# Routing attention with a spectral gate: the first mask made head by head, fewer idle products, and a new order of instructions

## The chip, the core and the metric

The kernel runs on one core of a Trainium2 chip. A core has five engines with instruction queues of their own: TensorE (PE, matrix products), VectorE (DVE), ScalarE (ACT), GpSimd (POOL) and SyncE (SP, which here only starts transfers). Sixteen DMA engines move data. Products land in PSUM, which has eight banks of 128 rows by 2 KB; everything else lies in SBUF. Each engine takes its instructions in the order in which they stand in the program, and an instruction that needs another engine's result waits for a semaphore. The metric is the device time of one execution in microseconds (us); lower is better. "Profile" means one execution recorded by the hardware profiler.

## What is computed

The reference, cut to what matters:

```python
q_assign = argmax(einsum('bhsd,hcd->bhsc', q_n, c_n), -1)     # 16 centroids per head
k_assign = argmax(einsum('bhsd,hcd->bhsc', k_n, c_n), -1)
mask = q_assign[:, :, :, None] == k_assign[:, :, None, :]
scores = where(mask, q @ k.T / sqrt(64), -1e9)
attn = exp(scores - max);  attn = attn / (attn.sum(-1) + 1e-9)
x = (attn @ v)                                                # (4, 768, 8 * 64)
x1, x2, x3 = split(x @ w_proj, 3)                             # 512 -> 3 * 512
y = x1 * irfft(rfft(x2) * rfft(filter)) * x3                  # along the sequence
out = y @ w_out                                               # (4, 768, 512) float32
```

There are 4 batches, 8 heads, 768 positions and 64 numbers per head. Every position is given to the nearest of 16 centroids, for its query and for its key; a query sees only the keys with the same centroid.

## The kernel before

The work is cut into eight groups n of four heads (batch n // 2, half n % 2), and each group into two pairs pr of two heads hp. `routing(n)` turns q and k of a group so that the 64 numbers of a head lie along the rows, multiplies with the normed centroids, takes the argmax, and makes a one-hot row block: 16 rows, one per centroid, which stand beside the 64 rows of q or k in the operands of the scores. With these rows a product of q and k comes out hugely negative where the centroids differ, so that the mask costs no work of its own. These operands are the tiles `aug`: `aug_97` is head 0 and `aug_98` head 1 of the first pair, `aug_99` and `aug_100` belong to the second pair, `aug_101` and `aug_102` to the third; then the three are used again in turn. In each, j = 0 is the query side and j = 1 the key side.

`attention(n, pr)` runs over six blocks sk of 128 keys. For each there are three score products ("thirds" of 512 columns: the first is head 0 alone, the second half of each head, the third head 1 alone; lines 156 and 158), three exponentials on ACT into a tile `p` (lines 690 and 693), one group of eight products with v (line 704), and a running sum of `p` for the denominator (lines 713 and 717, DVE or POOL). When two groups of a batch are done, `hyena` makes the projection, the spectral filter as products with cosine tables, the gates and the output product (lines 158, 455 and 838).

The first pair is a case of its own, `first_masks(0)`. Its start goes so: two waves of transfers bring q and k (line 295); PE turns them by products with the identity `ident` (line 602, three per PSUM bank); ACT or DVE copies each bank to `qkP` (lines 246 and 248 are the helper that copies); four products with the centroid matrix `cbd` give the similarities (line 502); ACT copies them to `sim`; PE turns them back (line 511); DVE takes the argmax in five instructions over 24 groups of 16 (lines 518 to 525: maximum, equal to it, times a falling weight so that the first of equal ones wins, maximum, equal to it), into the one-hot tile `oh`; PE turns this into rows (line 535) in two banks, one for j = 1 and one for j = 0, each with both heads; and four copies `put` (line 546 or the helper) write the rows to `aug_97` and `aug_98`. The bodies of q and k come to `aug` by the casts of `routing` on ACT, DVE or POOL. The second pair takes the same five instructions once more (`first_masks(1)`), then six turns (line 555), one write to `sim` (line 558) and four transfers by SP (line 487).

Before its first real product, PE runs idle products on a tile of ones (`warm`, with `awake` as one product, line 1101): ten ahead of everything, and one more ahead of each of the eight turns of the first group.

The order of all this isn't found at run time. `build` records each step as an `Op` with the engines that may do it, what it reads and what it writes. `arrange` then walks through the list `ORDER`: each number stands for a step (number // 5) and the engine that does it (number % 5), and the steps are issued in that order. `due` and the costs in an `Op` don't move anything here; only the list does. `arrange` also gives out the PSUM banks, the first free ones of its list, and decides by the step before whether a product is issued whole or as two halves of 64 columns. A step marked `lock` on POOL waits for the last step marked so on DVE.

## Time and profile before

| | us |
|---|---|
| median of 3 runs | 348.03 |
| lowest and highest run | 347.56, 348.55 |
| the profiled execution | 348.1 |
| its span, from the first to the last instruction | 346.3 |
| PE busy in the span | 336.8 |
| DVE busy | 327.6 |
| ACT busy | 274.2 |
| POOL busy | 135.1 |
| first exponential starts | 16.52 |
| first product with v starts | 19.62 |

A row of the timeline has the start in us, the length in us, the engine, the line, the operation and "out<-in" with the shape; "x3" means that three instructions are merged, and a bracket gives the idle time of the engine just ahead of it with what ended it. "PEld" is a weight load on TensorE, "SPq" and "ACTq" are the starts of transfers. Where two rows of an engine overlap a little, the next instruction entered while the one before was still finishing. In the table of stages each engine has its busy time with the number of instructions, then the granted clock of TensorE, the share of the DMA engines and their rate.

### The profile page before, as it was taken

To read this page: it belongs to the slowest core of one execution; us is meant where nothing else is said; L and a number is where in the kernel's file an instruction comes from. 1 tells how busy PE (TensorE), PEld (TensorE's weight loads), DVE (VectorE), ACT (ScalarE), POOL (GpSimd) and SP (SyncE) were. 2 spreads that over 40 slices of the span, in tenths; PEclk is the share of its full clock that TensorE was granted. 3 is DMA by queue.
4 is the path that set the end of the run, shared out by engine and by line. 5 is a ranking of instruction groups with operands and counts; after the bars stand their busy time and mean duration, and the time that the engine had idled before them with its cause. 6 is when DMAs were issued, how large, how long until landed. Compare 5 with 4: busy or idle time off the path is not lost.

```text
span 346.3 us, 8366 instructions
## 1 busy us (share of the span) xinstructions
PE 336.8 (97%) x3164; PEld 194.7 (56%) x3165; DVE 327.6 (95%) x438; ACT 274.2 (79%) x509; POOL 135.1 (39%) x161
## 2 busy tenths in 40 slices
PE   8899999999999999999999999999999999999994
PEld 4464465454455556655665656676455555576672
DVE  6899999999999999999999999999999999989992
ACT  7999999999799989887898797697998655524442
POOL 6423407004115447234702686126501161336740
PEclk9999999999999999999999999999999999999998
DMA  8979986775799997798969776998748321500124
GB/s 184 195 150 208 181 168 125 123 152 122 161 160 157 141 169 89 153 117 185 142 124 167 132 126 150 195 135 128 164 103 142 72 25 43 173 5 2 74 110 184
DMA packets 132052, 46.19 MB, mean 133 GB/s; under 512 B 119192, under 2 KB 124140, under 8 KB 132012
## 3 DMA queue, kind: packets, MB, share of 16 engines
q1 hardware_dynamic: 127884, 35.79, 49.9%
q0 software_dynamic: 2752, 8.98, 18.7%
q10 hardware_dynamic: 1376, 0.89, 0.8%
q8 instruction: 25, 0.41, 0.5%
q14 instruction: 15, 0.12, 0.1%
HBM read 31.59 MB, written 7.40 MB: 113 GB/s over the span
## 4 chain that ended last, share of the span: by engine, by line
PE 81%; ACT 8%; DVE 8%; issue 1%; ACTq 0%; DVEq 0%
PE bank L158 38%; PE pair L704 32%; PE bank L838 5%; PE bank L622 3%; DVE acc L717 2%; ACT aug L246 1%; PE bank L733 1%; DVE tm L868 1%; PE bank L455 1%; ACT p L693 1%; ACT qkP L246 1%; ACT sim L648 1%; DVE ohB L637 1%; DVE oh L635 1%; DVE mx L633 1%
## 5 line engine op out<-in xcount | busy, mean ns | idle before, releaser
L704 PE MATMUL pair<-p,vraw 128*64 128x385 f32 x768 | 142.1, 487 | 0.0
L693 ACT ACTIVATE p<-bank 128x512 f32<-128x512 f32 x192 | 108.6, 606 | 22.5 <-PE bank L158 19.8
L717 DVE TENSOR_TENSOR acc<-p,acc 128x1536 f32<-128x1536 f32 x64 | 112.9, 1765 | 2.6 <-ACT p L693 0.2
L158 PE MATMUL bank<-aug 128*64 128x512 bf16 (+1 forms) x738 | 83.7, 327 | 0.3 <-ACT p L693 0.2
L704 PEld LDWEIGHTS pair<-p,vraw 128*64 128x64 f32 x768 | 57.9, 136 | 42.6 <-issue 33.7
L158 PEld LDWEIGHTS <-aug 128*64 128x64 bf16 (+1 forms) x738 | 45.0, 109 | 36.7 <-issue 25.3
L754 POOL DMA_DIRECT2D acc<-acc x30 | 23.9, 796 | 98.4 <-DVE acc L717 61.4
L690 ACT ACTIVATE p<-bank 128x512 f32<-128x512 f32 x96 | 57.1, 609 | 5.4 <-PE bank L158 4.3
L158 PE MATMUL bank<-xT,wpj 128*64 128x384 bf16 x504 | 49.4, 326 | 0.0
L158 PEld LDWEIGHTS <-wpj 128*64 128x64 bf16 x504 | 30.9, 110 | 14.4 <-issue 4.6
L246 ACT CAST aug<-qkP 64x768 bf16<-64x768 f32 x46 | 37.7, 829 | 0.8
L713 POOL TENSOR_TENSOR acc<-p,p 128x1536 f32<-128x1536 f32 x7 | 24.3, 3474 | 29.6 <-DVE acc L717 27.8
L158 PEld LDWEIGHTS <-y 128*64 128x64 bf16 x488 | 24.6, 110 | 12.7 <-issue 4.1
L868 DVE TENSOR_TENSOR tm<-bank,hm 128x512 f32<-128x512 f32 x44 | 27.9, 681 | 1.1 <-PE bank L455 0.5
L158 PE MATMUL bank<-wout,y 128*64 128x512 bf16 (+1 forms) x200 | 23.9, 371 | 0.2 <-DVE y L964 0.2
L579 DVE STREAM_TRANSPOSE qkP<-qkraw 128x768 f32<-128x768 f32 x26 | 24.0, 953 | 0.0
L838 PE MATMUL bank<-wpj,xT 128*64 128x512 bf16 x192 | 22.8, 379 | 0.4 <-ACT tm L246 0.4
L872 POOL TENSOR_TENSOR y<-tm 128x512 bf16<-128x512 f32 x15 | 19.0, 1274 | 10.6 <-DVE tm L868 8.2
L964 POOL TENSOR_TENSOR y<-yy,x 128x768 bf16<-128x768 f32 x9 | 16.4, 1827 | 15.1 <-DVE acc L717 7.1
L246 ACT COPY x<-bank 128x384 f32<-128x384 f32 x27 | 13.1, 484 | 11.4 <-PE bank L158 10.6
L246 ACT COPY ob<-bank 128x512 f32<-128x512 f32 x22 | 12.8, 589 | 11.1 <-PE bank L158 9.4
L248 POOL CAST aug<-qkP 64x768 bf16<-64x768 f32 x15 | 12.5, 840 | 17.7 <-DVE acc L717 7.4
(175 smaller groups left out, 415.0 us busy)
## 6 DMA issues: line engine op xcount, KB each, us to landing
rb<-dr SPq DMA_DIRECT2D x30, 192.0 KB, 3.5
qkraw<-in_k_dram SPq DMA_DIRECT2D x55, 96.0 KB, 3.2
qkraw<-in_q_dram SPq DMA_DIRECT2D x55, 96.0 KB, 3.2
vraw<-in_v_dram SPq DMA_DIRECT2D x52, 96.0 KB, 3.2
out_dram<-ob SPq DMA_DIRECT2D x9, 512.0 KB, 3.2
acc<-acc POOLq DMA_DIRECT2D x10, 384.0 KB, 5.2
acc<-acc POOLq DMA_DIRECT2D x10, 192.0 KB, 4.0
y<-in_moe_filter_fft_dram SPq DMA_DIRECT2D x4, 384.0 KB, 4.9
```

The costliest lines, as they stand in the source:

```text
L158: T.nc.tensor.matmul(out[64 * i:64 * i + 64], lhsT[:, 64 * i:64 * i + 64], rhs, start=start, stop=stop)
L246: T.nc.scalar.copy(out, in_)
L579: op(("DVE", .96), lambda e, s=s, z=z, j=j: V().transpose(T.qkP[z // 2][:, ts(j, S)], T.qkraw[s][:].rearrange("p t h d -> p (t h d)") if j ...
L690: T.nc.scalar.activation(o, ap(h).rearrange("p (a b) -> p a b", a=2), Act.Exp, scale=0.125)
L693: T.nc.scalar.activation(flat(s)[:, lo:lo + 512], ap(h), Act.Exp, scale=0.125)
L704: T.nc.tensor.matmul(o[64 * hp:64 * hp + 64, ch, :385], T.vraw[vs][:, hp, sk * D:(sk + 1) * D], T.p[slots[sk]][:, hp, 384 * ch:384 * ch + ...
L713: alu(e).tensor_tensor(T.acc[os], T.p[slots[0]][:, :, :S], T.p[slots[1]][:, :, :S], op=Alu.add)
L717: T.nc.vector.tensor_tensor(T.acc[os], T.p[slots[sk]][:, :, :S], T.acc[os], op=Alu.add)
L754: op(("POOL", .8), lambda e, rows=rows: T.nc.gpsimd.dma_start(flat_()[:rows], flat_()[rows:2 * rows], accum_op=Alu.add), te, r=[], w=AK, b ...
L838: T.nc.tensor.matmul(ap(h)[64 * i:64 * i + 64], T.xT[xs][:, kt, c:c + 64], T.wpj[:, kt, DM:2 * DM], start=kt == 0, stop=kt == ND - 1)
L868: op(("DVE", .68), lambda e, i=i, cs=cs, r=r, h=h: T.nc.vector.tensor_tensor(T.tm[r][:, cs], ap(h), hmrow(i, (0, 2, 2, 3)[2 * r + cs]), op ...
L872: op({"POOL": 1.5, "DVE": .68}, lambda e, i=i, r=r: alu(e).tensor_tensor(T.y[:, i, r], T.tm[r][:, 0], T.tm[r][:, 1], op=Alu.add if r else ...
```

## The change

The change has four parts.

The argmax of the first pair is cut by heads. In place of five DVE instructions over 24 groups there are ten over 12 groups, five for each head; every second group belongs to a head (`hp::2`). The turns to rows are cut likewise: four banks of six products in place of two of twelve, so that each bank holds one head and one j. There are still four `put` copies.

The idle products are cut: `WARM` is 8 in place of 10, and the first four turns (query and key of the first pair, `z` 0 and 1) have no idle product ahead of them. Of 18 idle products 12 are left.

The keys of `mx` and `oh` are now per head for the first pair, and `both` in `routing` names all of them. This only keeps the dependencies right.

`ORDER` is a new list over the whole program, since the steps have new numbers and stand in another order. It also gives some steps to another engine: in all, ACT has 41 casts to `aug` in place of 46, DVE none in place of 2, and POOL 22 in place of 15; ACT has 3 of the zero fills of `aug` (line 1074, now 1080) in place of 1, and POOL 3 in place of 5; one `put` is on ACT, where all four were on DVE.

```diff
 ORDER = [
-    2, 179, 106, 28, 5, 171, 23, 32, 154, 161, 184, 18, 48, 169, 13, 98, 159, 37, 62, 51, 206, 66, 58, 267, 189, 272, 277, 149, 43, 112, 236, 117,
+    2, 154, 106, 13, 18, 5, 181, 159, 166, 98, 62, 149, 23, 164, 28, 37, 822, 179, 51, 103, 236, 267, 58, 207, 189, 76, 272, 277, 174, 66, 112, 43,
...
-WARM = 10
+WARM = 8
...
-        bc = lambda a: a.unsqueeze(2).to_broadcast([128, 24, NC])
-        op(("DVE", .55), lambda e: V().tensor_reduce(mx(), sv(), axis=AX, op=Alu.max), due + .5, r=[h], w=[("mx", pr)])
...
+        put_ = []
+        for hp in range(2) if pr == 0 else (None,):
+            N = 24 if hp is None else 12
+            k = ((pr,) if hp is None else (pr, hp))
+            part = (lambda x: x) if hp is None else (lambda x, hp=hp: x[:, hp::2])
+            bc = lambda a, N=N: a.unsqueeze(2).to_broadcast([128, N, NC])
+            D_ = (.55, .36) if hp is None else (.36, .26)
+            dd = due + .5 * (hp or 0)
+            op(("DVE", D_[0]), lambda e, part=part: V().tensor_reduce(part(mx()), part(sv()), axis=AX, op=Alu.max), dd + .5, r=[h], w=[("mx", *k)])
+            op(("DVE", D_[0]), lambda e, part=part, bc=bc: V().tensor_tensor(part(oh()), part(sv()), bc(part(mx())), op=Alu.is_equal), dd + .6,
+               r=[h, ("mx", *k)], w=[("oh", *k)], free=[h])
...
+            for j in (1, 0) if pr == 0 else ():
                 h2 = Bank("head")
-                def rows(e, j=j, h2=h2):
+                def rows(e, j=j, hp=hp, h2=h2):
                     o = ap(h2).bitcast(BF16)
                     for t in range(NT):
-                        for hp in range(2):
-                            T.nc.tensor.transpose(o[64 - 64 * hp:80 - 64 * hp, ts(t, 128)], oh()[:, at(t) + 2 * j + hp], T.identb)
+                        T.nc.tensor.transpose(o[64 - 64 * hp:80 - 64 * hp, ts(t, 128)], oh()[:, at(t) + 2 * j + hp], T.identb)
...
-                def tr(e, s=s, ch=ch, j=j, h=h):
-                    if n == 0:
+                def tr(e, s=s, ch=ch, z=z, h=h):
+                    if n == 0 and z > 1:
                         awake(h)
...
-        both = lambda x: [(x, 0), (x, 1)]
+        both = lambda x: [(x, 0, 0), (x, 0, 1), (x, 1)]
```

The new list shows in the instructions at three places. In these rows the line numbers of the changed kernel are higher (602 is 608, 502 stays, 518 is 525, 535 is 540, 546 is 551, 555 is 561, 693 is 699, 704 is 710). The names `bank_63` to `bank_68` and `bank_153`, `bank_154` are PSUM banks.

On DVE, the argmax of the first pair and the writes of its rows, before, up to the argmax of the second pair:

```order
L518 TENSOR_REDUCE mx<-bank_65 128x24
L519 TENSOR_TENSOR oh<-bank_65,mx 128x384
L521 TENSOR_TENSOR oh<-oh,revc 128x384
L523 TENSOR_REDUCE m_87<-oh 128x24
L525 TENSOR_TENSOR oh<-oh,m_87 128x384
L248 CAST aug_98<-qkP_113 64x768
L546 TENSOR_SCALAR aug_97<-bank_68 16x768
L248 COPY aug_97<-bank_153 16x768
L546 TENSOR_SCALAR aug_98<-bank_68 16x768
L518 TENSOR_REDUCE mx<-bank_154 128x24
L248 COPY aug_98<-bank_153 16x768
L519 TENSOR_TENSOR oh<-bank_154,mx 128x384
```

and after:

```order
L525 TENSOR_REDUCE mx<-bank_65 128x12 x2
L526 TENSOR_TENSOR oh<-bank_65,mx 128x12x16 x2
L528 TENSOR_TENSOR oh<-oh,revc 128x12x16 x2
L530 TENSOR_REDUCE m_87<-oh 128x12
L532 TENSOR_TENSOR oh<-oh,m_87 128x12x16
L530 TENSOR_REDUCE m_87<-oh 128x12
L532 TENSOR_TENSOR oh<-oh,m_87 128x12x16
L551 TENSOR_SCALAR aug_98<-bank_68 16x768
L551 TENSOR_SCALAR aug_97<-bank_154 16x768
L248 COPY aug_97<-bank_63 16x768
L525 TENSOR_REDUCE mx<-bank_66 128x24
L526 TENSOR_TENSOR oh<-bank_66,mx 128x384
```

The two heads go side by side up to the weighting; then head 1 (`aug_98`) is finished first and head 0 (`aug_97`) second. One cast and one of the four writes have left this stretch of DVE.

On ACT, from the copy of the first pair's similarities to the first exponential, before:

```order
L246 COPY sim<-bank_154 128x384
L246 CAST aug_97<-qkP_113 64x768
L373 ACTIVATE fw<-tm_136 128x2x192
L246 COPY qkP_114<-bank_63 128x384
L246 COPY qkP_114<-bank_66 128x384
L246 COPY qkP_114<-bank_64 128x384
L373 ACTIVATE fw<-tm_137 128x2x192
L246 CAST aug_100<-qkP_114 64x768
L246 COPY sim<-bank_67 128x384
L368 ACTIVATE ob_139<-tm_137 128x384
L693 ACT_TABLE_LOAD
L693 ACTIVATE p_103<-bank_66 128x512
```

and after:

```order
L246 COPY sim<-bank_154 128x384
L373 ACTIVATE fw<-tm_136 128x2x192
L375 ACTIVATE wout<-ob_138,half_pi 128x2x192
L373 ACTIVATE fw<-tm_137 128x2x192
L246 COPY qkP_114<-bank_66 128x384
L246 COPY qkP_114<-bank_67 128x384
L368 ACTIVATE ob_139<-tm_137 128x384
L246 CAST aug_100<-qkP_114 64x768
L246 COPY sim<-bank_64 128x384
L246 COPY aug_98<-bank_153 16x768
L699 ACT_TABLE_LOAD
L699 ACTIVATE p_103<-bank_67 128x512
```

One cast and one copy have left the stretch, one table of sines (line 375) and the write of head 1's key rows have come in.

On PE, the turns of the first pair up to the turn of the centroids, before (the rows of ten idle products ahead are left out):

```order
L1101 MATMUL bank_64<-wpj 128x512
L602 MATMUL bank_64<-ident,qkraw_91 128x128 x3
L1101 LDWEIGHTS wpj
L1101 MATMUL bank_65<-wpj 128x512
L602 MATMUL bank_65<-ident,qkraw_90 128x128 x3
L1101 LDWEIGHTS wpj
L1101 MATMUL bank_66<-wpj 128x512
L602 MATMUL bank_66<-ident,qkraw_91 128x128 x3
L1101 LDWEIGHTS wpj
L1101 MATMUL bank_67<-wpj 128x512
L602 MATMUL bank_67<-ident,qkraw_90 128x128 x3
L332 MATMUL bank_68<-ident,sd 64x128
```

and after, up to the first similarities (the rows of eight idle products ahead are left out):

```order
L608 MATMUL bank_64<-ident,qkraw_90 128x128 x3
L608 MATMUL bank_65<-ident,qkraw_90 128x128 x3
L608 MATMUL bank_66<-ident,qkraw_91 128x128 x3
L608 MATMUL bank_67<-ident,qkraw_91 128x128 x3
L332 MATMUL bank_68<-ident,sd 64x128
L1107 LDWEIGHTS wpj
L1107 MATMUL bank_153<-wpj 128x512
L608 MATMUL bank_153<-ident,qkraw_92 128x128 x3
L502 MATMUL bank_154<-qkP_113,cbd 32x384 x4
```

The four turns of the first pair stand without idle products between them, and the query is turned ahead of the key.

More of the change, by code (lines that the diff above doesn't have):

```diff
@@ L549, in first_masks, with put @@
-            return [got]
+                        T.nc.tensor.transpose(o[64 - 64 * hp:80 - 64 * hp, ts(t, 128)], oh()[:, at(t) + 2 * j + hp], T.identb)
+                op(("PE", .21), rows, dd + 1.0 + .1 * (1 - j), r=[("oh", *k), "identb"], w=[h2], alloc=h2, kind="sim")
+                def put(e, j=j, hp=hp, h2=h2):
+                    rs = slice(64 - 64 * hp, 80 - 64 * hp)
+                    o, x = T.augs[0][hp][j][rs], ap(h2).bitcast(BF16)[rs, :S]
+                    if j:
+                        copy(e, o, x)
+                    elif e == "ACT":
+                        T.nc.scalar.activation(o, x, Act.Copy, scale=BIG, bias=-BIG)
+                    else:
+                        V().tensor_scalar(o, x, BIG, -BIG, op0=Alu.mult, op1=Alu.add)
@@ L550, in first_masks @@
+                put_ = [op({"ACT": .8, "DVE": .55}, put, dd + 1.2 + .3 * hp, r=[h2, ("zero", 0, j)],
+                           w=[("augm", 0, hp, j)], free=[h2])]
+        if pr == 0:
+            return put_
         h2 = Bank("head")
```

31 lines of the change are left out of this document (7 added, 24 removed), and 158 rows, old and new, of the table ORDER.

## The prediction

> **What bounds the kernel now.** I read the page first, then the busy times by stage, the waits of PE, and the timeline of the first 25 us.
>
> ```profile
> span 346.3 us, 8366 instructions
> PE 336.8 (97%) x3164; PEld 194.7 (56%) x3165; DVE 327.6 (95%) x438; ACT 274.2 (79%) x509; POOL 135.1 (39%) x161
> ...
> L246 ACT CAST aug<-qkP 64x768 bf16<-64x768 f32 x46 | 37.7, 829 | 0.8
> ...
> L248 POOL CAST aug<-qkP 64x768 bf16<-64x768 f32 x15 | 12.5, 840 | 17.7 <-DVE acc L717 7.4
> ```
>
> ```profile
> core 0: us, PE busy (x) PEld busy (x) DVE busy (x) ACT busy (x) POOL busy (x), PEclk, DMA share, GB/s
> 0.00:10.00 10.00, 8.52 (x39) 4.30 (x39) 7.16 (x26) 7.64 (x15) 5.87 (x38) 1.00 0.79 179
> 10.00:20.00 10.00, 8.11 (x79) 5.15 (x78) 8.68 (x17) 9.84 (x20) 3.92 (x5) 1.00 1.06 207
> 20.00:60.00 40.00, 39.84 (x332) 21.80 (x330) 39.35 (x38) 38.32 (x70) 16.12 (x28) 1.00 0.86 164
> 60.00:140.00 80.00, 78.71 (x670) 41.00 (x668) 78.49 (x85) 73.58 (x137) 26.98 (x22) 1.00 0.82 140
> 140.00:320.00 180.00, 179.97 (x1771) 107.84 (x1769) 174.75 (x242) 134.12 (x249) 71.21 (x60) 1.00 0.64 119
> 320.00:347.00 27.00, 21.64 (x286) 14.64 (x282) 19.19 (x35) 10.70 (x23) 10.98 (x10) 0.95 0.31 118
> ```
>
> From 20 us on PE hardly rests: 0.16 us idle up to 60, 1.29 up to 140, 0.03 up to 320. So the time is three things: when PE's dense stretch begins, how much useful work is done by then, and the tail. DVE is nearly as full (78.49 of 80 us between 60 and 140), and ACT has 9.84 of 10 us between 10 and 20: ACT, not PE, carries the start.
>
> Since PE's useful work is the same before and after, an order can win at most those 1.5 us (0.16 + 1.29 + 0.03) in the body; it can lose any amount.
>
> **The start, step by step.**
>
> ```profile
> 4.29 0.83 ACT L1074 ACTIVATE aug<-ident 64x768 bf16<-64x768 f32 x1
> ...
> 4.67 0.22 DVE L319 TENSOR_REDUCE ss<-sd 128x1 f32<-128x64 f32 x1
> ...
> 5.02 0.69 ACT L357 ACTIVATE ob<-x,magic,s1t 128x384 f32<-128x384 f32 x1
> ...
> 9.18 0.62 ACT L375 ACTIVATE wout<-ob,half_pi 128x384 bf16<-128x384 f32 x1
> ...
> 10.13 0.48 ACT L246 COPY sim<-bank 128x384 f32<-128x384 f32 x1
> ...
> 10.51 0.83 ACT L246 CAST aug<-qkP 64x768 bf16<-64x768 f32 x1
> ...
> 11.32 0.56 DVE L518 TENSOR_REDUCE mx<-bank 128x24 f32<-128x384 f32 x1 [0.86 <-PE bank L511]
> ...
> 12.57 0.36 DVE L521 TENSOR_TENSOR oh<-oh,revc 128x384 bf16<-128x384 bf16 x1
> ...
> 13.55 0.56 DVE L525 TENSOR_TENSOR oh<-oh,m 128x384 bf16<-128x384 bf16 x1
> ```
>
> (a) The copy of the similarities on ACT, at 10.13. Ahead of it the new list has two zero fills more (line 1074, 0.83 each) and one L357 (0.69) and one L375 (0.62) less: 1.66 - 1.31 = +0.35. On DVE one L359 more stands ahead of the norms of the centroids. Instructions overlap at their ends (the zero fill at 4.29 has its successor at 5.02, 0.73 later), so I take +0.2; ends 0 (the wait for PE's similarities hides it) and +0.5.
>
> (b) The argmax. Five instructions ran from 11.32 to 14.11 (13.55 + 0.56). A reduction over 64 numbers takes 0.22 and over 384 takes 0.56, so over 192 it is 0.22 + 0.34 * 128 / 320 = 0.36 (an estimate from those two rows); the weighting, 0.36 whole, gives some 0.26. Ten halves are 8 * 0.36 + 2 * 0.26 = 3.40 against 2.59 for the five. But in the chain each step waited for the last to drain (2.79 from end to end for 2.59 of work), and with two heads side by side a neighbour fills that drain. Ends: +0.2 and +0.8; I take +0.35. This is the point of the change that looks wrong way round: the first score is of head 0, and head 0 is finished second. What is early is head 1, which nothing asks for first.
>
> ```profile
> 14.14 0.56 DVE L248 CAST aug<-qkP 64x768 bf16<-64x768 f32 x1
> ...
> 15.21 0.55 DVE L248 COPY aug<-bank 16x768 bf16<-16x768 bf16 x1
> 15.22 1.28 ACT L693 ACT_TABLE_LOAD   x1
> ...
> 16.26 0.54 DVE L518 TENSOR_REDUCE mx<-bank 128x24 f32<-128x384 f32 x1
> 16.52 0.60 ACT L693 ACTIVATE p<-bank 128x512 f32<-128x512 f32 x1
> ...
> 17.01 0.86 ACT L246 COPY qkP<-bank 128x384 f32<-128x384 f32 x2
> ...
> 18.42 0.59 ACT L690 ACTIVATE p<-bank 128x512 f32<-128x512 f32 x1
> 18.86 0.56 DVE L525 TENSOR_TENSOR oh<-oh,m 128x384 bf16<-128x384 bf16 x1
> ...
> 19.45 0.56 DVE L248 CAST aug<-qkP 64x768 bf16<-64x768 f32 x1
> ...
> 19.62 0.54 PE L704 MATMUL pair<-p,vraw 128*64 128x385 f32 x1
> ...
> 20.11 0.69 DVE L558 TENSOR_SCALAR sim<-bank,mka,mkb 64x768 bf16<-64x768 bf16 x1
> ```
>
> (c) The rows. Before, a cast and two writes stood between the argmax and the first score (14.14 to 15.76); after, three writes of the same size do. No difference. The first score is then some 0.5 later.
>
> (d) The first exponential, 16.52, began when the table load ended (15.22 + 1.28 = 16.50). Between the similarities' copy and that load ACT loses a cast (0.83) and a copy (0.43, half of 0.86), and gains L375 (0.62) and a write of 768 columns (0.83 at most, by the cast of 768): +0.2, with (a) +0.4. The first exponential comes at about 16.9. Then two copies (0.86) no longer stand together behind it, one goes behind each of the first two, so the third ends near 19.3 in place of 19.01: +0.3.
>
> (e) The second pair's argmax, 16.26 to 19.42. One write (0.54) and the cast of 14.14 are gone from it, against +0.5 of (a) and (b): it ends some 0.4 earlier, about 19.0.
>
> (f) PE. The new list puts the second pair's turns and the third block's scores ahead of the first product with v, and those scores need the bank that L558 frees: 19.0, then a cast (0.56), L558 (0.69) and two thirds give about 20.7, against 19.62 before. But by then PE has done two turns more, which ran at 24.12 before, and one third:
>
> ```profile
> 24.12 0.80 PE bank L602 x6
> ```
>
> That is 0.80 (0.65 without the drain) + 0.22, so PE stands 1.1 - 0.9 = +0.2 us behind. Ends: -0.4, if (a) and (b) are at their low ends, and +0.9, if both are high.
>
> **The idle products.**
>
> ```profile
> 1.12 4.87 PE L1101 MATMUL bank<-wpj 128*128 128x512 bf16 x11 [1.12 <-DVE wpj L1105]
> ...
> 6.41 0.38 PE L1101 MATMUL bank<-wpj 128*128 128x512 bf16 x1
> ...
> 6.96 0.38 PE L1101 MATMUL bank<-wpj 128*128 128x512 bf16 x1
> ...
> 9.22 0.85 PE L502 MATMUL bank<-qkP,cbd 128*32 128x384 f32 x8 [0.36 <-ACT ob L368]
> ...
> 10.66 0.55 PE L511 MATMUL bank<-ident,sim 128*128 128x128 f32 x3
> ...
> 11.59 0.38 PE L1101 MATMUL bank<-wpj 128*128 128x512 bf16 x1
> ```
>
> Eleven products fill 4.87 us, 0.44 each. From 6.41 a product and three turns together fit into 0.55. So PE runs at about half speed until some 6.2 us, though the granted clock reads 1.00 in the first 10 us as everywhere. Taking the products away saves nothing by itself, since ACT, and not PE, carries the start. Cost on the path: 0, as long as PE is fast when L502 comes at 9.2.
>
> [...]
>
> **The body.** Seven casts go to POOL (0.84 each), five leave ACT (0.83) and two DVE. ACT and DVE have PE's waits in their hands, so this may win some of the 1.5 us; a cast on POOL that comes late may cost more. I take 0; ends -1.2 and +2.5.
>
> **The tail.**
>
> ```profile
> 339.54 2.35 PE L158 MATMUL bank<-wout,y 128*64 128x256 bf16 x22 [0.25 <-DVE y L964]
> ```
>
> PE waits 0.25 us for DVE's last gate. In the new list DVE has eight instructions behind PE's next-to-last gate product where it had nine, so the wait goes: -0.2. What follows, PE's last product, a copy on ACT and a transfer, is of the same kind. Ends -0.3 and +0.3.
>
> **Sum.** +0.2 (start) + 0 (idle products) + 0 (body) - 0.2 (tail) = 0 against the profiled execution's 348.1, which has 1.8 us around its span and lies 0.07 over the median of 348.03. I predict 348.1. A change of less than 0.3%, about 1.04 us, can't be told from none by these measurements.
>
> **Rivals.**
>
> [...]
>
> *Late casts on POOL.* POOL's casts sat idle 17.7 us ahead, 7.4 of that for DVE's running sums, since a locked POOL step waits for DVE. Seven more such casts, and one that is needed by a score before it is done holds all of PE for up to a sum and a cast:
>
> ```profile
> L717 DVE TENSOR_TENSOR acc<-p,acc 128x1536 f32<-128x1536 f32 x64 | 112.9, 1765 | 2.6 <-ACT p L693 0.2
> ```
>
> That is 1.77 + 0.84 = 2.6. With half of one such wait and +0.2 from the start: 349.6. Against it: a cast is made a pair ahead.
>
> *DVE's relief carries through.* The second pair is ready 0.4 earlier, DVE has two casts less (1.1 us), ACT five; the start comes out at -0.2 and a good half of the body's 1.5 us of waits goes: 348.1 - 0.2 - 0.8 - 0.2 = 346.9. For it: DVE is 98% busy from 60 to 140, where PE's waits are. Against it: the first score is later.
>
> **Numbers.** Chances: no clear change 0.43; the gate 0.13; late casts 0.21; relief 0.23. The gate and late casts are over 0.3% but for a few hundredths, as is the relief on its side: faster 0.21, same 0.46, slower 0.33. The range runs from 346.6 (relief with the low end of the start) to 350.4 (late casts at full price, or the gate through L511 and part of the scores); the gate shut into the dense stretch, and one or two waits more in the body, are left out, under 2 in 10. The likeliest case's own range is 347.1 to 349.1.
>
> **What the new profile would show.** The first exponential at 16.7 to 17.2, the ten halves in 3.0 to 3.3 us, the second pair's argmax done near 19.0, the first product with v at 20.5 to 20.9, L502 at 0.85. PE's idle time from 60 to 140 us tells the body. I am wrong if L502 takes over 1.2, if a score waits for a cast on POOL, or if PE is dense well before 20.4.

## The result, and the profile after

The changed kernel takes 351.65 us (median of 4 runs, 351.31 to 352.19) against 348.02 for the kernel before beside it: a ratio of 1.0098, 95% interval 1.0084 to 1.0113. That is 3.6 us slower, where I had forecast 348.1 and a range up to 350.4. Its profiled execution took 351.31 with a span of 349.6. All ratios in this document are made from fast runs alone; one slow run each of e3_start (356.97 us) and e7_mend (500.39) still counts in their medians in the table further down.

Line numbers are those of the changed kernel from here on (602 is 608, 622 is 628, 693 is 699, 704 is 710, 964 is 970, 1090 is 1096, 1101 is 1107). The page's first part, then the table of stages for the changed kernel:

```profile
span 349.6 us, 8373 instructions
...
PE 338.5 (97%) x3158; PEld 197.3 (56%) x3158; DVE 326.7 (93%) x441; ACT 271.9 (78%) x504; POOL 143.8 (41%) x168
```

```profile
20.00:60.00 40.00, 38.55 (x319) 18.24 (x318) 38.02 (x35) 37.73 (x68) 17.03 (x27) 1.00 0.95 163
60.00:82.00 22.00, 21.85 (x186) 10.48 (x183) 21.74 (x21) 21.13 (x41) 4.80 (x3) 1.00 0.66 131
82.00:142.00 60.00, 58.75 (x494) 31.12 (x492) 57.34 (x68) 49.70 (x91) 24.98 (x23) 1.00 0.89 145
142.00:320.00 178.00, 177.95 (x1755) 107.65 (x1752) 171.88 (x235) 133.66 (x249) 73.58 (x61) 1.00 0.64 118
```

The same table for the kernel before, in the two stretches that the prediction did not cut so:

```profile
60.00:82.00 22.00, 21.42 (x180) 10.43 (x178) 21.44 (x20) 21.06 (x41) 4.71 (x3) 1.00 0.70 140
82.00:142.00 60.00, 59.29 (x521) 31.88 (x517) 58.82 (x66) 54.47 (x100) 22.27 (x19) 1.00 0.86 140
```

PE has been idle for 1.45 us between 20 and 60 us (0.16 before) and for 1.25 between 82 and 142 us (0.71 before); from 142 to 320 us it is idle for 0.05. The start, in the timeline of the changed kernel:

```profile
1.12 3.59 PE L1107 MATMUL bank<-wpj 128*128 128x512 bf16 x8 [1.12 <-DVE wpj L1111]
...
5.62 2.85 PE L608 MATMUL bank<-ident,qkraw 128*128 128x128 f32 x12 [0.92 <-DMA qkraw<-in_q_dram]
...
8.90 0.85 PE L608 MATMUL bank<-ident,qkraw 128*128 128x128 f32 x3
...
9.68 0.89 PE L502 MATMUL bank<-qkP,cbd 128*32 128x384 f32 x8
...
10.64 0.48 ACT L246 COPY sim<-bank 128x384 f32<-128x384 f32 x1 [0.30 <-PE bank L502]
10.73 0.49 PE L608 MATMUL bank<-ident,qkraw 128*128 128x128 f32 x3
...
11.83 0.62 DVE L525 TENSOR_REDUCE mx<-bank 128x12 f32<-128x192 f32 x2
...
14.40 0.36 DVE L532 TENSOR_TENSOR oh<-oh,m 128x192 bf16<-128x192 bf16 x1
...
17.13 0.60 ACT L699 ACTIVATE p<-bank 128x512 f32<-128x512 f32 x1
...
18.65 0.56 DVE L532 TENSOR_TENSOR oh<-oh,m 128x384 bf16<-128x384 bf16 x1
...
21.16 0.54 PE L710 MATMUL pair<-p,vraw 128*64 128x385 f32 x2
```

Three turns still take 0.85 us at 8.90 and 0.49 at 10.73: PE came to full speed some 3 us later than before, where three turns take 0.79 at 5.79 and 0.49 at 6.63. The ten halves last from 11.83 to 14.76, 2.93 us. The first product with v comes at 21.16, 1.54 us later than before. Two turns (0.65) and a third of scores (0.22) more have been done by then, so PE stands 0.67 us behind.

The stalls between 20 and 60 us, from the timeline of DVE and PE:

```profile
35.98 0.98 DVE L643 STREAM_TRANSPOSE ohB<-oh 128x768 bf16<-128x768 bf16 x1
37.02 0.52 PE L158 MATMUL bank<-ohB,tri 128*64 128x384 bf16 x4 [0.51 <-DVE ohB L643]
48.67 0.41 PE L158 MATMUL bank<-aug 80*64 80x512 bf16 x2 [0.38 <-DVE h L435]
56.49 1.84 DVE L585 STREAM_TRANSPOSE qkP<-qkraw 128x768 f32<-128x768 f32 x2 [0.90 <-DMA qkraw<-in_k_dram]
58.38 0.85 PE L628 MATMUL bank<-qkP,cbd 128*32 128x384 f32 x8 [0.47 <-DVE qkP L585]
```

The third one comes from a transfer. The list of transfers of the changed kernel between 46 and 58 us shows, with the size of each and the median time from issue to landing, what ran beside it; the last row is the same kind over the whole program:

```profile
qkraw<-in_k_dram SPq DMA_DIRECT2D x4, 96.0 KB, 7.5
...
wpj<-in_moe_w_proj_dram POOLq DMA_DIRECT2D x1, 384.0 KB, 6.9
wout<-in_moe_w_out_dram POOLq DMA_DIRECT2D x1, 128.0 KB, 4.1
```

```profile
qkraw<-in_k_dram SPq DMA_DIRECT2D x54, 96.0 KB, 3.3
```

The last part of the projection's weights, fetched at 37.15 before, is fetched at 49.03 now, in the window in which keys are loaded; keys that land in 3.3 us over the whole program take 7.5 here (3.0 in the same window of e9_mend2 below, which fetches no weights then). The tail, in the timeline of the changed kernel and then of the kernel before (the last transfer that it issues):

```profile
341.95 2.68 PE L158 MATMUL bank<-wout,y 128*64 128x256 bf16 x28 [0.48 <-DVE y L970]
...
345.28 0.34 ACTq L1012 DMA_DIRECT2D out_dram<-ob  x1
```

```profile
342.55 0.34 ACTq L1006 DMA_DIRECT2D out_dram<-ob  x1
```

PE waits 0.48 for the last gate (0.25 before) and has 28 products behind it where it had 22 (2.68 us and 2.35). From its last product to the end of the span it is 349.6 - 344.63 = 4.97, and 346.3 - 341.89 = 4.41 before.

The profile's account: start 0.67; PE's idle time from 20 to 320 us 2.90 against 1.48, so 1.42; tail 0.23 + 0.33 + 0.56 = 1.12. Together 3.2 of the 3.3 us between the spans. That this sum closes is luck: the runs below give the start and the tail less than this, and the body twice as much.

### The profile page after: what moved, and what is told of

It reads as the page before. It is cut to its first block, busy times and chain, and to the rows that moved or that the text cites. A ratio compares the mean times of both kernels' runs of the same rounds, so it can differ in the third digit from the quotient of the medians.

```text
span 349.6 us, 8373 instructions
## 1 busy us (share of the span) xinstructions
PE 338.5 (97%) x3158; PEld 197.3 (56%) x3158; DVE 326.7 (93%) x441; ACT 271.9 (78%) x504; POOL 143.8 (41%) x168
## 4 chain that ended last, share of the span: by engine, by line
PE 76%; DVE 12%; DMA 4%; issue 3%; SPq 1%; POOL 1%; ACT 1%; DVEq 0%; ACTq 0%; POOLq 0%
PE bank L158 36%; PE pair L710 26%; PE bank L844 6%; DVE acc L723 4%; PE bank L628 2%; DMA qkraw<-in_k_dram 2%; DVE acc L719 1%; DMA rb<-dr 1%; PE bank L608 1%; POOL acc L719 1%; PE bank L455 1%; DVE xT L810 1%; DMA qkraw<-in_q_dram 1%; DVE ohB L643 1%; DVE sim L633 1%
## 5 line engine op out<-in xcount | busy, mean ns | idle before, releaser
L723 DVE TENSOR_TENSOR acc<-p,acc 128x1536 f32<-128x1536 f32 x64 | 112.6, 1760 | 3.0
L158 PE MATMUL bank<-aug 80*64 80x512 bf16 (+1 forms) x744 | 83.5, 326 | 0.9 <-DVE h L435 0.4
L710 PEld LDWEIGHTS pair<-p,vraw 128*64 128x64 f32 x768 | 56.8, 137 | 43.2 <-issue 35.5
L158 PEld LDWEIGHTS <-aug 80*64 80x64 bf16 (+1 forms) x744 | 44.8, 109 | 40.9 <-issue 28.9
L158 PE MATMUL bank<-xT,wpj 128*64 128x384 bf16 x496 | 48.6, 326 | 0.0
L158 PEld LDWEIGHTS <-wpj 128*64 128x64 bf16 x496 | 32.2, 110 | 13.5 <-issue 5.8
L246 ACT CAST aug<-qkP 64x768 bf16<-64x768 f32 x41 | 33.8, 829 | 1.1 <-DVE qkP L585 0.2
L158 PEld LDWEIGHTS <-y 128*64 128x64 bf16 x488 | 26.3, 110 | 10.5 <-issue 2.9
L248 POOL CAST aug<-qkP 64x768 bf16<-64x768 f32 x22 | 18.2, 837 | 29.2 <-PE bank L158 10.2
L970 POOL TENSOR_TENSOR y<-yy,x 128x768 bf16<-128x768 f32 x10 | 18.2, 1823 | 19.9 <-DVE xT L810 14.0
L810 DVE SCALAR_TENSOR_TENSOR xT<-osb,rb 128x384 bf16<-128x384 f32 x30 | 17.8, 634 | 1.3 <-DMA rb<-dr 1.1
```

The costliest lines, as they stand in the source:

```text
L158: T.nc.tensor.matmul(out[64 * i:64 * i + 64], lhsT[:, 64 * i:64 * i + 64], rhs, start=start, stop=stop)
L246: T.nc.scalar.copy(out, in_)
L710: T.nc.tensor.matmul(o[64 * hp:64 * hp + 64, ch, :385], T.vraw[vs][:, hp, sk * D:(sk + 1) * D], T.p[slots[sk]][:, hp, 384 * ch:384 * ch + ...
L723: T.nc.vector.tensor_tensor(T.acc[os], T.p[slots[sk]][:, :, :S], T.acc[os], op=Alu.add)
L810: T.nc.vector.scalar_tensor_tensor(o[:, :, ::-1] if c else o, osv()[:, :, cols], eps(), r, op0=Alu.add, op1=Alu.mult)
```

## Experiments

**Theories.** *The list*: the loss is made by the new order behind the start, through DVE's late results. *The start*: fewer idle products and the halves make a late start, and the rest follows from it. *Late casts on POOL*, the prediction's rival, is tried further down.

In the diffs `new` is the changed kernel's list and `old` is the list of before in the new numbering, each step of the first pair's argmax and rows standing twice, for head 0 and then head 1. Both lists set the engine of each step too. `a[:k] + rest(b)` is the first k entries of `a`, then what is left in the order of `b`. Where nothing else is said a kernel has the change's eight idle products. The table has all runs; each ratio is to the kernel before, timed beside it.

| kernel | what | median us | ratio | 95% interval |
|---|---|---|---|---|
| e1_idle | kernel before, idle products cut | 347.97 | 1.0000 | 0.9986 to 1.0014 |
| e2_split | old list, halves, 18 idle products | 347.93 | 0.9998 | 0.9987 to 1.0009 |
| e3_start | new start, old rest | 349.08 | 1.0016 | 0.9999 to 1.0032 |
| e4_rest | old start, new rest | 350.42 | 1.0067 | 1.0048 to 1.0087 |
| e5_tail | old, new from 310 us | 348.79 | 1.0013 | 0.9996 to 1.0031 |
| e6_early | old, new in 22 to 62 us | 349.62 | 1.0039 | 1.0020 to 1.0057 |
| e10_early2 | old, new in 20 to 82 us | 349.45 | 1.0039 | 1.0017 to 1.0062 |
| e8_mid | old, new in 62 to 310 us | 351.84 | 1.0094 | 1.0073 to 1.0116 |
| e11_mid2 | old, new in 82 to 142 us | 351.74 | 1.0092 | 1.0071 to 1.0113 |
| e12_late | old, new in 142 to 300 us | 349.33 | 1.0013 | 0.9997 to 1.0030 |
| e7_mend | new, stalls mended, hw moved | 354.41 | 1.0159 | 1.0129 to 1.0189 |
| e9_mend2 | new, stalls mended | 351.45 | 1.0075 | 1.0053 to 1.0098 |
| e13_casts | old, casts on the new engines | 355.89 | 1.0208 | 1.0181 to 1.0234 |
| e14_inject | old, three causes put in | 349.89 | 1.0040 | 1.0027 to 1.0053 |
| e15_reverse | new, old in 20 to 82 us | 350.72 | 1.0070 | 1.0058 to 1.0083 |
| e17_reverse3 | new, old in 82 to 142 us | 349.95 | 1.0044 | 1.0022 to 1.0067 |
| e16_reverse2 | new, old in 20 to 142 us | 348.78 | 1.0010 | 0.9993 to 1.0027 |
| e18_idle | the same with 18 idle products | 347.58 | 0.9970 | 0.9952 to 0.9988 |

### The parts alone

```diff
# e1_idle, in the kernel before
-WARM = 10
+WARM = 8
...
-                    if n == 0:
+                    if n == 0 and z > 1:
                         awake(h)
# e2_split, in the changed kernel
-ORDER = new
+ORDER = old
-WARM = 8
+WARM = 10
...
-                    if n == 0 and z > 1:
+                    if n == 0:
                         awake(h)
# e3_start
-ORDER = new
+ORDER = new[:170] + rest(old)
# e4_rest
-ORDER = new
+ORDER = old[:170] + rest(new)
```

> The kernel before with one part of the change: eight idle products in the first wait and none ahead of the first four turns; list and argmax as before. Two theories. The list: the 3.6 us come from the order of the rest of the program, and the idle products cost the start alone; TensorE is slow for some 3 us longer and the first turns take about 0.9 us more, of which ACT hides most: 348.0 to 348.6. The start: the slow turns move everything behind them; the first exponential comes 0.6 us later as in the changed kernel, the stalls of the body follow from it, and the time is 349.5 to 351.5.

> The argmax and the rows by heads alone: the list of before, in which each of the five steps stands twice, head 0 and then head 1, and each turn to rows twice; eighteen idle products. The list: ten halves take 2.9 to 3.1 us in place of 2.79, and the time is that of before plus 0 to 0.4, 348.0 to 348.4. The start: halves that fill DVE delay the second pair's argmax and with it the third block's scores, and the time is 348.6 to 349.5.

> The changed kernel with its own first 170 steps (to about 22 us: idle products, halves, rows, the first product with v) and from there the steps that are left in the order and on the engines of before. The list: the start is late by 0.3 us of work and the rest runs as before, 348.0 to 348.9. The start: the rest inherits the late start and its stalls, 350.5 to 352.

> The other way about: the first 170 steps in the order of before (with the halves side by side and eight idle products), then what is left in the new list's order. The list: the stalls of the body and the longer tail are there, 350.5 to 351.8, TensorE idle over 1 us between 20 and 60 us. The start: with the start of before the body runs dense, 348.0 to 349.

Idle products and halves cost nothing alone, to 0.14% and 0.11%. The new start costs 0.16%, at the edge of what can be told; the new list behind the start of before costs 0.67%. So the theory of the start falls: most of the loss is there without the new start.

The two starts of PE that eight idle products allow are both there to be seen, in the timeline of PE of e1_idle (lines of the kernel before), and of e4_rest (lines 10 lower than the changed kernel's):

```profile
5.67 1.17 PE L602 MATMUL bank<-ident,qkraw 128*128 128x128 f32 x9 [0.95 <-DMA qkraw<-in_k_dram]
```

```profile
5.51 2.79 PE L598 MATMUL bank<-ident,qkraw 128*128 128x128 f32 x12 [0.80 <-DMA qkraw<-in_k_dram]
```

After the same eight products (1.12 to 4.71 us in both) nine turns take 1.17 us in the one and twelve take 2.79 in the other. In 17 profiles of kernels with eight idle products the slow turns (0.85 for three) were over by 6.8 us, if there were any, in 8 and lasted beyond 9.4 in 9; with eighteen they were over by 6.7 in all 3. The first exponential of the start of before came at 16.38 to 16.41 in the early ones and at 16.64 to 17.34 in the late ones.

The two groups lie over 2.6 us apart after the same block of 3.59 us, and what decides between them is not shown.

### Where in the list

```diff
# e5_tail
-ORDER = new
+ORDER = old[:1790] + rest(new)
# e6_early
-ORDER = new
+ORDER = (old[:170] + rest(new))[:400] + rest(old)
# e8_mid
-ORDER = new
+ORDER = (old[:400] + rest(new))[:1790] + rest(old)
```

> The order of before (halves side by side, eight idle products) for all but the last 161 of 1951 steps; those, from about 310 us, in the order and on the engines of the new list. If the tail has a price of its own: TensorE has 28 products behind the last gate in place of 22, with 0.5 us more of waits ahead of them and 0.5 us more behind its last product, so plus 1.2 to 1.7 us: 349.2 to 349.9. If the tail is only late because what stood before it was late: 347.9 to 348.3.

> The new list from step 170 to step 400 alone (about 22 to 62 us), the order of before ahead of it and behind it. If the stalls of 20 to 60 us keep their price: plus 1.0 to 1.5 us, 349.0 to 349.5, with TensorE idle for more than 1 us in that stretch. If the rest of the program takes such stalls back, because ACT or DVE bounds it anyway: 347.8 to 348.4.

> The new list from step 400 to step 1790 alone (about 62 to 310 us), the order of before ahead of it and behind it. By the traces TensorE loses 0.9 us more there up to 140 us and 1.0 less behind: 347.5 to 348.3. If the casts that moved to POOL or the later transfers of this stretch carry the loss: 349 to 350.

The stretch from 22 to 62 us costs what was expected, 0.39%. The tail costs 0.13%, with an interval that holds zero, and so less than the profile's 1.12 us; the 0.56 of that behind the last product lie within what single profiles vary by (below). The middle missed its expectation by 3 us, and its waits show why. PE's longest waits in e8_mid:

```profile
PE bank L158 <- DVE ohB L643: 1.3, 2, 0.9
```

The longest stands at 66.05, just behind the seam at 62 us; neither whole list has a wait of PE over 0.1 us between 60 and 68 us. At step 400 the two lists are 9 steps apart, so steps of one have to catch up there. I then cut where they are 1 to 4 steps apart:

```diff
# e10_early2
-ORDER = new
+ORDER = (old[:141] + rest(new))[:513] + rest(old)
# e11_mid2
-ORDER = new
+ORDER = (old[:513] + rest(new))[:871] + rest(old)
# e12_late
-ORDER = new
+ORDER = (old[:871] + rest(new))[:1747] + rest(old)
```

> The new list from step 141 to step 513 alone (about 20 to 82 us), cut where the two lists stand at nearly the same point (4 and 3 steps apart), the order of before ahead and behind. The list theory: the stalls of 20 to 60 us and no more, plus 0.9 to 1.4: 348.9 to 349.5. If stalls in this stretch are taken back by what follows: 347.9 to 348.4.

> The new list from step 513 to step 871 alone (about 82 to 142 us), cut likewise. The list theory: TensorE's waits for h, for the gates and for the exponentials at 108.8 and 136.4 us cost 0.8 to 1.2: 348.8 to 349.3. If these only stand where the trace of before has its own at other places: 347.9 to 348.4.

> The new list from step 871 to step 1747 alone (about 142 to 300 us), cut likewise (4 steps and 1 step apart). By the traces this stretch runs 0.6 to 1.0 us better in the new list: 347.0 to 347.6, which would beat both kernels. If that was only a matter of where the same products fall in the windows: 347.8 to 348.5.

The early stretch gives 0.39% again with other seams. The late one is no gain (0.13%, with an interval that holds zero). The stretch from 82 to 142 us gives 0.92%, three times what I expected; its longest waits are four for an exponential, the longest of them at 147.00, again behind a seam:

```profile
PE bank L158 <- ACT p L699: 1.2, 4, 0.6
```

The five stretches that were put in alone add up to 1.73% (start 0.16, 0.39, 0.92, 0.13, tail 0.13), the whole change to 0.98%, so the seams cost something too. To tell a stretch's own cost from a seam's, I took the stretches out of the new list instead; the seams then make the result worse, not better.

```diff
# e15_reverse
-ORDER = new
+ORDER = (new[:141] + rest(old))[:513] + rest(new)
# e17_reverse3
-ORDER = new
+ORDER = (new[:513] + rest(old))[:871] + rest(new)
# e16_reverse2
-ORDER = new
+ORDER = (new[:141] + rest(old))[:871] + rest(new)
```

> The changed kernel with the order of before from step 141 to step 513 (about 20 to 82 us). If that stretch costs what it cost in the list of before (0.39%), the time falls by 1.4 from 351.65: 350.0 to 350.6. If a seam made that cost: 351.3 to 352.

> The changed kernel with the order of before from step 513 to step 871 alone (about 82 to 142 us); the stalls of 20 to 60 us stay. If the two stretches cost apart from each other (0.28% and 0.60% by the last two runs): 351.65 less 2.1, 349.3 to 350. If the second stretch only carried on what the first had made late: 351 to 352.

> The changed kernel with the order of before from step 141 to step 871 (about 20 to 142 us), so with the new start, the new stretch from 142 us on and the new tail. If 82 to 142 us costs another 0.8 to 1.2 by the list itself: 348.8 to 349.6, which is the start and the tail. If the 0.9% that this stretch showed was a matter of its seams: 350 to 351.

Without 20 to 82 us the ratio falls from 1.0098 to 1.0070, without 82 to 142 us to 1.0044, without both to 1.0010. That is 0.28%, 0.54% and 0.88%, so the two add up (0.82), and with both out no difference from the kernel before is left that can be told. The loss lies in the order from 20 to 142 us. The table of stages for e16_reverse2:

```profile
20.00:60.00 40.00, 39.84 (x339) 20.74 (x339) 39.42 (x38) 39.00 (x72) 15.67 (x27) 1.00 0.87 169
60.00:82.00 22.00, 21.44 (x184) 10.54 (x180) 21.46 (x20) 21.07 (x41) 4.11 (x3) 1.00 0.67 130
82.00:142.00 60.00, 59.29 (x518) 31.91 (x516) 58.83 (x67) 54.03 (x99) 22.21 (x19) 1.00 0.87 141
```

The stalls are gone with the stretch, with the new start ahead of it. But 0.88% is 3.1 us, and PE's idle time from 20 to 142 us has fallen by 2.85 - 1.43 = 1.42 only. Part of the rest is spacing. Take for every product the distance from its start to the next product's, less the median of that distance for its shape in the three profiles together: from 82 to 142 us this adds up to 11.5 us in the kernel before, 13.2 in the changed one and 11.9 in e17_reverse3, while the idle times differ by half a microsecond. Products that stand farther apart read as busy, since their ends are modelled. What sets them apart I did not follow.

### What in the list: mending and putting in

I mended the three stalls of 20 to 60 us in the new list:

```diff
# e7_mend: steps moved in `new`
+ 283 (product with v) ahead of 251, 254 (the two products of ohB)
+ 341 (last part of the projection's weights) behind 342 (the third); 346 (output's weights) 100 steps later
+ 408 (L585) behind 151 (the filter's h)
+ 141 (the filter's weights hw, L407) ahead of 59 (the fills L381)
# e9_mend2: the same without the last
- 141 (the filter's weights hw, L407) ahead of 59 (the fills L381)
```

> The changed kernel with its three stalls of 20 to 60 us mended one by one: the product with v that stands behind the two products of ohB stands ahead of them; the last part of the projection's weights is fetched behind the third in place of 12 us later, and the first part of the output's weights later, so that neither shares the DMA engines with the keys that L585 waits for; the transposition L585 stands behind the spectral filter's h in place of ahead of it, and the filter's weights hw ahead of the casts that POOL does. If each stall has its own cause at its own place, TensorE's idle time from 20 to 60 us falls from 1.45 us to under 0.5 and the time by 1.0 to 1.6: 350.0 to 350.7. If DVE's or ACT's sum of work is what is missing, the stalls come back elsewhere: 351.2 to 352.

> The run with three mends once more, with the filter's weights hw left where the changed kernel has them (behind the two zero fills L381): the product with v goes ahead of the two products of ohB, the fetches of weights go out of the window in which the keys land, L585 goes behind the filter's h. If the stalls at 36.0, 47.9 and 57.4 us each have their own cause, TensorE's idle time from 20 to 60 us is under 0.6 us (1.45 in the changed kernel) and the time 0.9 to 1.6 us below the changed kernel's 351.65: 350.0 to 350.8. If the stalls come back elsewhere because DVE or ACT has no room: 351.2 to 352.2.

The first was a mistake, and a telling one. DVE, POOL and PE in the timeline of e7_mend, and POOL's row of the same five instructions in the kernel before:

```profile
36.45 3.39 DVE L415 TENSOR_TENSOR uv<-y,y 128x1536 bf16<-128x1536 f32 x2
...
37.97 5.48 POOL L407 TENSOR_SCALAR hw<-ph 128x3 f32<-128x3 f32 x5
...
39.76 3.61 DVE L723 TENSOR_TENSOR acc<-p,acc 128x1536 f32<-128x1536 f32 x2
...
43.64 0.62 PE L158 MATMUL bank<-uv,fw 128*64 128x512 bf16 x4 [2.58 <-POOL wout L381]
```

```profile
35.69 1.42 POOL L407 TENSOR_SCALAR hw<-ph 128x3 f32<-128x3 f32 x5
```

Five instructions of three columns took 5.48 us beside four DVE instructions of two operands (a sum and a difference, L415, and two running sums, L723), 1.42 in the kernel before, and the tiny fills L381 queued behind them, which the spectral filter's products wait for, held PE for 2.58 us.

POOL's five end at 43.45, when DVE's four have ended at 43.37; that DVE's work slows POOL's is my reading of these rows, and how it does so is not shown.

With that move left out (e9_mend2) the stalls for the keys and for ohB are gone, but PE's idle time has not fallen. Its waits from 20 to 60 us and its stage:

```profile
PE bank L158 <- DVE h L435: 0.4, 1, 0.4
PE bank L466 <- ACT p L699: 0.4, 1, 0.4
PE pair L710 <- ACT osb L726: 0.3, 1, 0.3
PE bank L158 <- POOL wout L381: 0.2, 1, 0.2
```

```profile
20.00:60.00 40.00, 38.37 (x319) 18.32 (x319) 37.85 (x36) 37.12 (x68) 16.10 (x27) 1.00 0.84 160
```

It is idle for 1.63 us where the changed kernel has 1.45. The ratio of 1.0075 can't be told from the changed kernel's 1.0098 (the intervals overlap). So I did not win the stretch back step by step: the wait for h stayed, and three new waits, two of them for ACT, took the place of the other two. The opposite test puts causes into the list of before; and the rival with the casts comes with it:

```diff
# e13_casts, in `old`: the casts to aug from entry 141 on
-  step s on the engine of before
+  step s on the engine that `new` gives it      (14 casts change engine)
# e14_inject: steps moved in `old`
+ 251, 254 (the two products of ohB) ahead of 283 (product with v)
+ 341 (last part of the projection's weights) to entry 317, 346 (output's weights) to entry 298, as in `new`
+ 141 (hw) behind 59 (L381)
```

> The order of before with halves and eight idle products, and in it the casts from step 141 on done by the engines of the new list, at the same places of the order: fourteen casts change engine, in sum more on POOL and fewer on ACT. The rival of the prediction (late casts on POOL): a score waits for a cast on POOL and TensorE with it, plus 0.7 to 1.7: 348.8 to 349.8. If the casts are no matter: 347.9 to 348.4. If the relief of ACT is worth something: 347.0 to 347.7.

> The order of before with halves and eight idle products, and in it only three moves towards the new list: the two products of ohB ahead of two products with v, the last part of the projection's and the first of the output's weights fetched later and earlier into the window in which the keys of the third group land, the filter's weights hw behind the zero fills L381. If each is a cause of its own, TensorE's idle time from 20 to 60 us goes from 0.2 to over 1.2 us and the time up by 1.0 to 1.6: 349.0 to 349.7. If these places are only where a shortage of time on DVE and ACT shows, they cost little in a list that has the time: under 0.5 us of idle time, 347.9 to 348.5.

e14_inject costs 0.40%, as much as the whole stretch of the new list. Its stages:

```profile
20.00:60.00 40.00, 39.42 (x330) 21.03 (x329) 38.57 (x36) 37.87 (x70) 17.23 (x27) 1.00 0.84 159
60.00:82.00 22.00, 20.87 (x174) 10.16 (x170) 20.72 (x20) 20.36 (x39) 3.61 (x4) 1.00 0.73 143
```

The idle time is 0.58 and 1.13 us where the kernel before has 0.16 and 0.58: only half of the extra 0.97 stands in the stretch of the moves, the other half behind it. Two waits make it up, in PE's timeline of e14_inject:

```profile
37.59 0.52 PE L158 MATMUL bank<-ohB,tri 128*64 128x384 bf16 x4 [0.48 <-DVE ohB L643]
...
80.45 0.85 PE L739 MATMUL bank<-acc,ones 128*32 128x384 f32 x8 [0.61 <-DVE acc L723]
```

The first is the stall that the first move was to make; the other two moves show no stall at their places, and the idle time stayed under the 1.2 us expected from 20 to 60. The three moves together are enough to cost what this stretch costs; that they are what costs it in the new list is not shown, since mending all but hw there won nothing that can be told.

e13_casts is the worst of all, 7.6 us. Its longest wait, less than half of that (the rest I did not follow), and what POOL does ahead of it:

```profile
PE bank L158 <- POOL wout L381: 3.1, 1, 3.1
```

```profile
32.29 3.99 POOL L248 CAST aug<-qkP 64x768 bf16<-64x768 f32 x3
...
39.31 4.24 POOL L407 TENSOR_SCALAR hw<-ph 128x3 f32<-128x3 f32 x5
```

More casts on POOL without a new order push hw from 35.69 us to 39.31, where it takes 4.24 us in place of 1.42, and the fills L381 to 44.17 behind it, and PE waits 3.1 us for two fills of 0.14. So late work on POOL does hold PE, at a place that the prediction hadn't named. In the changed kernel L381 comes at 41.57, ahead of hw, and no product waits for it; there it is DVE that waits for hw, 0.51 us ahead of L433 at 44.32.

### The better version

```diff
# e18_idle: e16_reverse2 with
-WARM = 8
+WARM = 10
...
-                    if n == 0 and z > 1:
+                    if n == 0:
                         awake(h)
```

The late gate, in what was expected, is the slow turns that last beyond 9.4 us; from e9_mend2, where they were over early, to the changed kernel the first exponential moves by 0.44 us (16.69 to 17.13).

> The changed kernel with the order of before from step 141 to step 871, as in the last run but one, and all eighteen idle products (ten, and one ahead of each of the eight turns). If the late gate costs half of 0.45 us on the average: 0.2 below that run, 348.0 to 348.7, which the interval can't tell from it, with the slow turns over by 6.6 us in the profile. If more idle products hold TensorE and the copies behind it: 348.9 to 349.5.

This kernel beats both: 347.58 against 348.37 beside it, 0.9970 with an interval of 0.9952 to 0.9988. It has the halves, the new start, the order of before from 20 to 142 us, and the new order behind that. Its twelve executions have spans of 345.2 to 346.7, the twelve of e16_reverse2, with eight idle products, 345.1 to 347.8: the best case is the same, and the worst is 1.1 us better. In the list of before the same cut cost nothing (e1_idle) and made the spans no wider (346.1 to 347.9, against 345.6 to 347.2 in e2_split with eighteen). The two were timed on different occasions besides, so how much of the 0.40% between their ratios the idle products bring stays open. Which of e18_idle's other parts is worth something is open too: alone none of them gained (start 1.0016, halves 0.9998, 142 to 300 us 1.0013, tail 1.0013).

## Why the prediction was wrong

**The start: +0.2 forecast, 0.67 in this profile, 0.16% (0.6 us) by e3_start.** The steps came out nearly as written, and best where PE was fast early. Three rows of e9_mend2, which has the changed kernel's start:

```profile
16.13 0.34 PEld L156 LDWEIGHTS <-aug 80*128 80x128 bf16 x3 [0.35 <-POOL aug L248]
...
16.69 0.60 ACT L699 ACTIVATE p<-bank 128x512 f32<-128x512 f32 x1
...
20.73 0.54 PE L710 MATMUL pair<-p,vraw 128*64 128x385 f32 x2
```

(a) The similarities' copy, forecast +0.2, came at 10.64 (+0.51), just past the upper end, because PE's slow turns delayed it (10.22 in e9_mend2, where they were fast). (b) The halves took 2.93 us, 0.14 over the five whole ones, where I had taken 0.35 with a low end of 0.2: the neighbour seems to fill the drain better than I took it to. (c) and (d) The first exponential, forecast 16.9, came at 16.69 or 17.13, on either side. (e) The second argmax, forecast 19.0, ended at 19.21. (f) The first product with v, forecast 20.7, came at 20.73 or 21.16. Of what I named as signs against me, L502 over 1.2 us didn't come in the changed kernel (0.89), nor a dense PE before 20.4. A score that waits for a cast on POOL did come: the first score's weights wait 0.35 us for one, at 16.57 in the changed kernel as at 16.13 in the row above. It is a small matter, since a score waits 0.94 us for such a cast in the kernel before too, at 17.41; as a sign it was badly chosen. And three of my sums don't close. (e) gives 18.8 by its own terms. The low end of the start is some -0.15 and not -0.4, as (a) and (b) at their low ends take 0.35 from the +0.2. Late casts at their full price are 348.1 + 2.6 = 350.7, above the range's end of 350.4.

**The idle products: 0 forecast.** Right for the list of before (1.0000), and the reason holds in the main: L502 takes 0.85 to 1.08 us in 16 of the 17 profiles with eight idle products and 1.30 in e10_early2. That PE is slow for longer came in 9 of 17 profiles (slow turns beyond 9.4 us), but moved the first exponential by 0.2 to 1.0 us (0.44 between 16.69 and 17.13) and the time not by the 1.8 that I had put on that case: PE was fast before the first scores (three turns in 0.49 at 10.73 in the changed kernel, the first score at 16.60).

**The body: 0 forecast, ends -1.2 and +2.5. This is the step that failed.** Taking its part from 20 to 142 us out of the new list moves the time by 0.88%, 3.1 us, more than the end I gave it. I had written that an order can lose any amount, but had looked only at how many casts change engine and costed the new order as such at nothing. But PE, DVE and ACT are 96 to 100% busy from 20 to 60 us in the kernel before, and 91 to 99% from 82 to 142, so a list has little slack to move things in: two products ahead of a third, one fetch of weights 12 us later, a few tiny instructions behind a fill. Moves like these were to be read in the comparison of the two lists, and e14_inject shows that three of them together cost 0.40%. I read that comparison at the start and the end only. Which moves make the larger part of the loss, 0.54% from 82 to 142 us, stays open: none was tried there one by one, and the sign that I had named for the body, PE's idle time from 60 to 140 us, went only from 1.29 to 1.40.

**The tail: -0.2 forecast, ends -0.3 and +0.3.** The wait for the last gate didn't go; it grew from 0.25 to 0.48, and six more products stood behind it. I had counted DVE's instructions ahead of the last gate (eight for nine) and not PE's behind it. By e5_tail it costs 0.13% (-0.04 to 0.31), 0.45 us, which the 0.33 us of the six products and the 0.23 of the wait would explain; the rest in the profile is the last transfer.

**The rivals.** The gate, in the chances and at the range's upper end, is the case in which PE is still at half speed when L502 comes. No run shows a gate; the profiles show slow turns (0.85 for three) until beyond 9.4 us in 9 of 17, and L502 at 0.89 in the changed kernel. The bounds I had for that case, 349.5 to 352, hold the measured time, but by luck: the start, where it was to act, costs 0.6 us. Late casts on POOL, at 349.6, stand 2 us below it, and no cast on POOL holds a score back after the first one in the changed kernel. The relief (346.9) is nearly what e18_idle shows, 0.30% or 1.0 us beside the 1.2 that I had written, but that is luck too: the waits that it was to take away are still there, with PE idle for 1.77 us from 20 to 320 us against 1.48 in the kernel before. That the time would end slower had a chance of 0.33.

## What to carry to other kernels

Where three engines are full at once, cost a new order by reading it against the old one over the whole full stretch, on every queue, POOL's and the transfers' too; count what each engine has behind the last wait as well as ahead of it. To find where a new order loses, exchange stretches in both directions, because a seam can cost nearly as much as the thing that was looked for (0.92% put in, 0.54% taken out, though the lists stood only 3 and 4 steps apart at the cuts). And don't expect a stall that the trace shows to be worth its length when it is mended: of three mended stalls two went and other waits came, while the whole stretch put back won nearly all of it.

## What the runs showed that was not expected

Behind eight idle products of 3.59 us TensorE is at full speed (0.49 us for three turns, 0.85 when slow) by 6.8 us in 8 of 17 profiles and only after 9.4 us in 9, while the granted clock of the first 10 us reads 1.00 in 16 of them (0.92 in e13_casts). Five POOL instructions of 128 x 3 take 1.42 us in the kernel before, 2.60 in the changed kernel, 4.24 in e13_casts and 5.48 in e7_mend. In e7_mend, beside four of DVE's two-operand instructions (3.39 and 3.61 us for two each), two of the five took 0.22 and 0.30 us and the other three 1.67 to 1.70, about as long as one of DVE's there. A 96 KB load of keys that lands in 3.3 us takes 7.5 when 512 KB of weights are fetched through POOL's queue in the same 12 us. And from PE's last product to the end of the span it is 4.0 to 4.3 us in 14 of 20 profiles, but 4.97 in the changed kernel's and 5.4 in e15_reverse's, which have the order of e18_idle, with its 4.0, at their end: that part of a difference between two single profiles is not the list's.
